# Tile 0 of a two-layer kernel: its last column group as seven quarter products, with another order of weight loads and of the second layer

## The chip, the cores and the metric

The kernel runs on one core of one Trainium2 chip. The metric is the device time of one execution in microseconds (us). Before the change the median of three runs is 261.32 us (261.23 to 261.98). A difference of about 0.3% (0.8 us) is what can be told from no change.

## What is computed

Linear attention without softmax over 8 batches of 8 heads (576 positions, 64 features), a normalisation of each output row, and two dense layers with a gate between them:

```python
kv  = einsum('bhsd,bhse->bhde', k, v)
out = einsum('bhsd,bhde->bhse', q, kv)
x   = out / sqrt(mean(out*out, -1) + 1e-6) * g_norm   # rows of 8 heads x 64 = 512 features
h   = x @ w_in            # 4608 x 512  times 512 x 2048
g   = h * sigmoid(1.702 * h)
y   = g @ w_out           # 4608 x 2048 times 2048 x 512
```

Inputs and output are float32 in HBM; the kernel works in float16 with float32 sums in PSUM.

## The kernel before

**Tiles.** The 4608 rows are worked in nine tiles of 512: tile t (0 to 7) takes positions 0 to 511 of batch t, and tile 8 the remaining 64 positions of all batches. While a tile goes through the two layers, the attention of the next batch is spread between its matmuls. Every engine's order is written out by hand: `layers` (L789) runs the first layer, then the second, and after step i of either it calls the units that the main loop (L978 to L1059) registered with `at1(i, ...)` and `at2(i, ...)`. Nothing is reordered later, so each engine works through its instructions in the order of the calls.

**Tiles 1 to 8** use a Strassen-like scheme in both layers. The two operands are cut in quarters, and seven products of quarters take the place of eight. In the first layer `SevenIn` (L546) does it for a group of four 128-wide columns of the hidden layer (i, i+1, i+8, i+9): products 1 to 7 of four matmuls with 256 columns each. Products 1, 6, 7 and 4 add up in one PSUM bank, x; product 2 goes into bank y, which starts as ScalarE's or VectorE's copy of x after product 1 (L604); 5 and 3 go into bank z, and a copy of z after product 5 is kept in SBUF as s5 (L606). After products 5 and 6 VectorE adds x and s5 into z (L608); after product 7 it adds x to s5 (L610). So product 7, which goes on adding to x, waits until L608 has read x. The gates (gelu, ScalarE, L574) read y after product 2, z after 3, x after 4, and s5 after L610. The operands are sums of quarters of the weights (`w_in_sums`, L504, into `ws`) and of the input (`Sums.form`, L522, into `xS`), formed on VectorE.

**Tile 0** uses no such scheme. Its first layer takes the 16 columns one by one, four matmuls of 512 columns each (`Hidden.mm`, L484), with a gelu on ScalarE behind each column (L496). The first six columns (0, 1, 2, 3, 8, 9) stand between the pieces of batch 0's attention (L892 to L914); `first_columns` (L806) does the other ten in the order 10, 11, 4, 5, 6, 12, 13, 7, 14, 15. The second layer, `project_all` (L816), is 64 steps of one matmul with 512 columns, step (mo, fo) adding column fo of the hidden layer times row block fo of w_out to output block mo. Two of its four accumulators come from the PSUM pool ps_h (three banks, tag hT), two from ps_o.

**Batch 1's attention** stands in tile 0's second layer, as units at steps: `pack_q` (VectorE puts q in order, L420), `q` (four transposes on PE into a ps_a bank, then ScalarE's copy, L425), `kv` (12 small matmuls per pair of heads, L248), `out` (one matmul, then ScalarE's square, L299), `ss` (one matmul that sums the squares into a ps_h bank, then ScalarE's reciprocal square root `rs`, L358), `apply` (VectorE multiplies into xT, L370). Gelu and the reciprocal square root lie in different ScalarE table sets; `preload_act_table_set` (step 4) loads one ahead of its use, and where an activation needs a set that isn't there, the compiler puts a load ahead of it. xT must be there when tile 1 begins.

**Loads.** All big loads go through GpSimd's queue (POOL), in the order of the calls: the rest of batch 0, w_in in seven pieces (L180 to L186, the last two being columns 4 to 7 and 12 to 15), then w_out and batch 1 in turn (L915 to L925). Eight of them are under way at a time: the ninth is issued when the first has landed. Since tile 1 on wants w_in multiplied by g_norm (`scale_w_in`, L203) and tile 0 unscaled, VectorE scales each part of w_in after tile 0 has used it and then forms the `ws` sums.

Of the kernel before, what the change touches and what calls it, by code (L numbers as in the profile page):

```python
# [16 lines left out]
def kernel(  # L17
# [10 lines left out]
    nc = tc.nc  # L28
# [14 lines left out]
    PE_ = 96  # L43
    NJ = S // PE_
    GROUP = 6
    COLS = (0, 1, 2, 3, 8, 9, 10, 11, 4, 5, 6, 12, 13, 7, 14, 15)
    assert PE_ * NJ == S and PE_ % 32 == 0

    const = ctx.enter_context(tc.tile_pool(name="const", bufs=1))
# [144 lines left out]
    def load_w_out(f0, f1):  # L194
        nc.gpsimd.dma_start(
            out=w_out_sb[:, f0:f1, :],
            in_=moe_w_out[f0 * P : f1 * P, :].rearrange("(fo ki) n -> ki fo n", ki=P),
        )
# [302 lines left out]
        lower = slice(KH + k.start, KH + k.stop)  # L501
        return w[:, k, f], w[:, lower, f], w[:, k, hi], w[:, lower, hi]

    def w_in_sums(g0, g1):  # L504

        f = slice(2 * g0 * P, 2 * g1 * P)
        a11, a12, a21, a22 = quarters(w_in_sb, f, slice(0, KH))
        s = [ws[:, n, :, f] for n in range(4)]
        nc.vector.tensor_add(s[0], a21, a22)
        nc.vector.tensor_sub(s[1], s[0], a11)  # L510
        nc.vector.tensor_sub(s[2], a11, a21)
        nc.vector.tensor_sub(s[3], a12, s[1])

    class Sums:

# [273 lines left out]
    def layers(t, units1, units2):  # L789
        hid = d0 if t == 0 else Hidden(t)  # L790
        seven = Seven(t, hid.gT) if t else None
        left = hid_seven(t, hid, seven, units1) if t else first_columns(hid, units1)
        osbs[t] = opool.tile([P, 4, DM], F32, name="osb", tag="osb")
        if t:
            todo = {n: [lambda x=x: seven.sums(*x) for x in xs] for n, xs in plan(t).later.items()}
            for n, us in units2.items():
                todo.setdefault(n, []).extend(us)
            for n, us in left.items():
                todo[n] = us + todo.get(n, [])
            seven.run(todo)  # L800
        else:
            project_all(hid.gT, units2)
        if t < B and t not in HALVED:
            store(t, 0, J)

    def first_columns(hid, units):  # L806

        for i, fo in enumerate(COLS):
            if i >= GROUP:
                for ko in range(KO):  # L810
                    hid.mm(ko, fo)
                hid.gate(fo)
            for u in units.get(i, ()):
                u()

    def project_all(gT, units):  # L816

        os = {}

        def project(mo, fo):  # L820
            if fo == 0:
                pool, tag = (ps_h, "hT") if mo < 2 else (ps_o, "o")
                os[mo] = pool.tile([P, DM], F32, name="o", tag=tag)
            nc.tensor.matmul(  # L824
                os[mo],
                gT[:, fo, mo * P : (mo + 1) * P],
                w_out_sb[:, fo, :],
                start=(fo == 0),
                stop=(fo == FO - 1),
            )  # L830
            if fo == FO - 1:
                copy = nc.scalar.copy if mo % 2 else nc.vector.tensor_copy
                copy(osbs[0][:, mo, :], os[mo])

        steps = [(mo, 4 * i + k) for i in range(3) for mo in range(4) for k in range(4)]
        steps += [(mo, f + k) for f in (12, 14) for mo in range(2) for k in range(2)]
        steps += [(mo, 12 + k) for mo in (2, 3) for k in range(4)]
        for n, (mo, fo) in enumerate(steps):
            project(mo, fo)
            for u in units.get(n, ()):  # L840
                u()
# [69 lines left out]
    for fo in COLS[4:GROUP]:  # L911
# [5 lines left out]
    load_w_out(4, 8)  # L917
    early_load("k", 1, 0, 2)
    load_w_out(8, 10)
    load_w_out(10, 12)  # L920
    early_load("v", 1, 0, 2)
    load_w_out(12, 14)
    early_load("k", 1, 2, NPAIR)
    early_load("v", 1, 2, NPAIR)
# [1 line left out]

    made = {}
    osbs = {}
    SECOND = Plan(
# [48 lines left out]
    for t in range(NT):  # L978
# [11 lines left out]

        if t == 0:
            for l in range(2):
                at1(6, nc.vector.memset, kvd[l], 0.0)
            at1(7, scale_w_in, 0, 4)
            at1(7, w_in_sums, 0, 2)
            at1(8, start, 1)
            at1(12, scale_w_in, 4, 6)
            at1(12, w_in_sums, 2, 3)
            at1(13, load_q, 2)
            at2(4, nc.scalar.preload_act_table_set, "abs_reciprocal_sqrt_and_small")  # L1000
            at2(18, weight_sum, 0, 0, HF)
            at2(18, scale_w_in, 6, 8)
            at2(18, w_in_sums, 3, 4)
            for c in range(NPAIR):
                at1(12, of(1, "pack_q", c))
                at2(9 + 3 * c, of(1, "q", c))
                at2((36, 37, 49, 50)[c], of(1, "kv", c))
                at2((41, 43, 54, 55)[c], of(1, "out", c))
                at2((45, 50, 58, 60)[c], of(1, "ss", c))
                at2((48, 52, 58, 62)[c], of(1, "apply", c))  # L1010
            for n in range(1, 4):
                at2(19, weight_sum, n, 0, 4)
                at2(38, weight_sum, n, 4, 6)
            at2(39, load_kv, 2, 0, H // 2, False)
            at2(51, clear_rest)
            at2(51, load_kv, 2, H // 2, H)

            def first_sum():
                made[1] = Sums(1, xT[1])
# [70 lines left out]
```

## Time and profile before

| | |
|---|---|
| median of three runs | 261.32 us |
| the profiled execution, its own time | 262.05 us |
| its span, first to last instruction | 260.3 us |
| around the span | 1.75 us |
| granted TensorE clock | 0.997 |
| tile 0's first layer (PE, from column 0's last quarter) | 16.99 to 28.21 us |
| tile 0's second layer with batch 1's attention | 28.21 to 47.52 us |
| tile 1's first product | 47.52 us |

Times in the views are microseconds from the span's start. A row of the timeline gives the start, the length of a run of like instructions, the engine, the line, output and inputs, their shape and count, and in brackets the engine's idle time ahead of it with what ended it. Matmuls overlap, so a run's length is longer than its distance to the next row: where PE is busy, the distance between starts is the price of a run. In the waits view a line gives who waited for whom, and the total, the count and the longest.

### The profile page before, as it was taken

What the parts mean: (1) busy time and instruction counts of PE and PEld (TensorE: products, weight loads), DVE (VectorE), ACT (ScalarE), POOL (GpSimd) and SP (SyncE); (2) the same over time, 40 slices, a digit from 0 to 9 for tenths busy, and PEclk for the clock granted to TensorE, in tenths of its full rate; (3) what the DMA queues carried; (4) which work ended last, traced back from release to release, by engine and by line L of the source; (5) the groups of instructions that cost most, each with busy time, mean ns of one, the idle gap of its engine ahead of it and who ended that gap; (6) DMA issues with size and microseconds to landing.
All of it is one profiled execution on the core that took longest, in us unless ns stands there. A gap on an engine that the chain in (4) does not pass through costs nothing.

```text
span 260.3 us, 6081 instructions
## 1 busy us (share of the span) xinstructions
PE 252.1 (97%) x2475; PEld 205.9 (79%) x2475; DVE 194.0 (75%) x350; ACT 174.1 (67%) x313; POOL 56.4 (22%) x85
## 2 busy tenths in 40 slices
PE   8899989999999999999999999999999999999992
PEld 2444544788988988898889888988899888888882
DVE  1656566899968986898689958995899578467831
ACT  2487714988649964996499649964897569737810
POOL 8963335107034002500160017200000000000000
PEclk9999999999999999999999999999999999999998
DMA  7999999999999969993799869998601620021005
GB/s 172 194 193 204 203 203 196 248 154 138 175 147 183 224 90 160 160 209 62 169 90 231 115 159 121 232 111 145 156 3 23 153 91 3 0 103 60 4 0 161
DMA packets 69886, 35.42 MB, mean 136 GB/s; under 512 B 39330, under 2 KB 67746, under 8 KB 69602
## 3 DMA queue, kind: packets, MB, share of 16 engines
q0 software_dynamic: 39056, 18.19, 55.8%
q1 hardware_dynamic: 30480, 16.45, 30.2%
q8 instruction: 19, 0.31, 0.5%
q10 hardware_dynamic: 322, 0.39, 0.5%
q14 instruction: 9, 0.07, 0.1%
HBM read 36.70 MB, written 9.44 MB: 177 GB/s over the span
## 4 chain that ended last, share of the span: by engine, by line
PE 84%; DMA 10%; POOL 4%; issue 0%; DVE 0%; POOLq 0%
PE h L594 38%; PE o L716 38%; DMA vbuf<-in_v_dram 6%; DMA w_in_sb<-in_moe_w_in_dram 4%; PE o L824 2%; PE outR L308 2%; PE kvp L236 2%; POOL w_in_sb L170 1%; POOL qraw L99 1%; POOL kraw L101 1%; POOL vbuf L101 1%; PE ss L356 1%; PE kvp L248 1%; PE outT L281 0%; PE outT L285 0%
## 5 line engine op out<-in xcount | busy, mean ns | idle before, releaser
L574 ACT ACTIVATE gT<-h 128x512 f16<-128x512 f32 x96 | 52.8, 604 | 5.4 <-PE h L594 5.4
L594 PEld LDWEIGHTS <-ws 128*128 128x128 f16 x512 | 50.1, 98 | 5.8
L716 PEld LDWEIGHTS <-gS 128*128 128x128 f16 x512 | 49.7, 98 | 5.8
L594 PE MATMUL h<-xS,ws 128*128 128x256 f16 x384 | 52.2, 273 | 0.0
L716 PE MATMUL o<-tw,gS 128*128 128x256 f16 x384 | 46.4, 273 | 0.0
L594 PEld LDWEIGHTS <-w_in_sb 128*128 128x128 f16 x384 | 37.1, 98 | 4.7
L716 PEld LDWEIGHTS <-gT 128*128 128x128 f16 x384 | 37.0, 98 | 4.0
L716 PE MATMUL o<-w_out_sb,gT 128*128 128x256 f16 x256 | 33.5, 273 | 0.0
L594 PE MATMUL h<-xT,w_in_sb 128*128 128x256 f16 x224 | 31.9, 273 | 0.0
L691 DVE TENSOR_TENSOR osb<-o,qf 128x512 f32<-128x512 f32 (+1 forms) x25 | 16.7, 669 | 14.7 <-PE o L716 11.9
L608 DVE TENSOR_TENSOR h<-h,s 128x512 f32<-128x512 f32 x32 | 22.2, 698 | 6.7 <-PE h L594 5.5
L113 POOL DMA_DIRECT2D kraw<-in_k_dram x7 | 6.0, 852 | 92.7 <-PE kvp L236 87.4
L610 DVE TENSOR_TENSOR s<-h,s 128x512 f32<-128x512 f32 x32 | 22.1, 691 | 4.1 <-PE h L594 3.3
L646 DVE TENSOR_TENSOR gS<-gT 128x512 f16<-128x512 f16 (+2 forms) x32 | 21.7, 685 | 0.6 <-ACT gT L574 0.6
L574 ACT ACTIVATE gT<-s 128x512 f16<-128x512 f32 x32 | 19.8, 628 | 2.6 <-DVE s L610 2.6
L986 ACT ACT_TABLE_LOAD x15 | 19.2, 1283 | 0.3
L358 ACT ACTIVATE rs<-ss,eps_t 128x512 f32<-128x512 f32 (+1 forms) x14 | 8.2, 597 | 16.6 <-PE ss L356 16.6
L745 POOL DMA_DIRECT2D out_dram<-osb x2 | 1.1, 554 | 84.1 <-DVE osb L691 84.1
L594 PE MATMUL h<-xS,w_in_sb 128*128 128x256 f16 x128 | 18.9, 273 | 0.0
L544 ACT COPY h<-h 128x512 f32<-128x512 f32 x27 | 15.7, 585 | 2.1 <-PE h L594 2.0
L594 PE MATMUL h<-xT,ws 128*128 128x256 f16 x112 | 16.8, 273 | 0.0
L544 ACT COPY s<-h 128x512 f32<-128x512 f32 x18 | 10.6, 588 | 8.8 <-PE h L594 8.2
(105 smaller groups left out, 374.2 us busy)
## 6 DMA issues: line engine op xcount, KB each, us to landing
out_dram<-osb SPq DMA_DIRECT2D x12, 512.0 KB, 3.1
kraw<-in_k_dram POOLq DMA_DIRECT2D x5, 512.0 KB, 8.2
vbuf<-in_v_dram POOLq DMA_DIRECT2D x5, 512.0 KB, 11.5
qraw<-in_q_dram POOLq DMA_DIRECT2D x4, 512.0 KB, 13.6
out_dram<-osb SPq DMA_DIRECT2D x2, 1024.0 KB, 5.2
qbuf<-in_q_dram POOLq DMA_DIRECT2D x3, 512.0 KB, 12.7
w_in_sb<-in_moe_w_in_dram POOLq DMA_DIRECT2D x2, 512.0 KB, 10.4
w_out_sb<-in_moe_w_out_dram POOLq DMA_DIRECT2D x2, 512.0 KB, 14.9
```

Source lines behind the costliest of these rows:

```text
L101: nc.gpsimd.dma_start(out=raw[n][0:PE_, c0:c1, :].rearrange("p c (l x) -> p (c l) x", l=2), in_=early_src(n, b, c0, c1),)
L113: nc.gpsimd.dma_start(out=kv_rows[n][:, h0 * RW : h1 * RW].rearrange("p (h x) -> p h x", x=RW), in_=srcs[n][b, h0:h1, 0:SM, :].rearrange(" ...
L358: nc.scalar.activation(rs[:, 0:n], t[:, 0:n], AFT.Abs_reciprocal_sqrt, bias=eps_t, scale=1.0 / D)
L544: (nc.vector.tensor_copy if engine == "D" else nc.scalar.copy)(to, src)
L574: nc.scalar.activation(self.gT[:, to, n * TH : (n + 1) * TH], src, AFT.Gelu_apprx_sigmoid)
L594: nc.tensor.matmul(bank[name][:, a], w, x, start=(p in (1, 5) and a == 0 and k == 0), stop=(k == KH - 1), skip_group_check=True,)
L608: nc.vector.tensor_add(bank["z"], bank["x"], self.s5)
L610: nc.vector.tensor_add(self.s5, bank["x"], self.s5)
L646: op(s[:, n, lo], a, b)
L691: nc.vector.tensor_add(o, ps, self.kept[with_][:, m])
L716: nc.tensor.matmul(o, a, w, start=(p in (1, 2, 5) and i == 0 and (mo == 0 or split)), stop=(i == HF - 1), skip_group_check=True,)
L986: u2.setdefault(i, []).append(lambda: f(*args))
```

## The change

Tile 0's columns 6, 7, 14 and 15 are no longer done one by one but as one group of `SevenIn`, with all its banks x and z from ps_a, y from ps_h, and both copies (x to y, z to s5) on ScalarE. `first_columns` now works through 10, 11, 4, product 1, 5, product 2, 12, 13, products 5, 6, 7; products 3 and 4 are units of the second layer at steps 3 and 7. The gate of product 2 stands behind that of column 12, the gates of products 4 and 7 behind product 4. The group's sums come first from unscaled weights (`w_in_sums(3, 4)` at step 7 of the first layer), and are formed again from scaled ones later. Two of the sums for groups 0 and 1, the clearing of kvd, the packing of q, the scaling of the later parts and batch 2's q load move to later units. The load of v for batch 1's first four heads moves ahead of that of w_out's rows 10 and 11. The second layer takes row blocks 0 to 3 and 4 to 7 for all four outputs, then 8 to 15 two at a time, and batch 1's units stand at other steps.

```diff
--- before.py
+++ after.py
@@ -43,7 +43,8 @@
     PE_ = 96
     NJ = S // PE_
     GROUP = 6
-    COLS = (0, 1, 2, 3, 8, 9, 10, 11, 4, 5, 6, 12, 13, 7, 14, 15)
+    COLS = (0, 1, 2, 3, 8, 9)
+    COLS_LATER = (10, 11, 4, "1", 5, "2", 12, 13, "5", "6", "7")
     assert PE_ * NJ == S and PE_ % 32 == 0
 
     const = ctx.enter_context(tc.tile_pool(name="const", bufs=1))
@@ -501,15 +502,19 @@
         lower = slice(KH + k.start, KH + k.stop)
         return w[:, k, f], w[:, lower, f], w[:, k, hi], w[:, lower, hi]
 
-    def w_in_sums(g0, g1):
+    def w_in_sums(g0, g1, which=range(4)):
 
         f = slice(2 * g0 * P, 2 * g1 * P)
         a11, a12, a21, a22 = quarters(w_in_sb, f, slice(0, KH))
         s = [ws[:, n, :, f] for n in range(4)]
-        nc.vector.tensor_add(s[0], a21, a22)
-        nc.vector.tensor_sub(s[1], s[0], a11)
-        nc.vector.tensor_sub(s[2], a11, a21)
-        nc.vector.tensor_sub(s[3], a12, s[1])
+        for n in which:
+            op, a, b = (
+                (nc.vector.tensor_add, a21, a22),
+                (nc.vector.tensor_sub, s[0], a11),
+                (nc.vector.tensor_sub, a11, a21),
+                (nc.vector.tensor_sub, a12, s[1]),
+            )[n]
+            op(s[n], a, b)
 
     class Sums:
 
@@ -799,19 +804,43 @@
                 todo[n] = us + todo.get(n, [])
             seven.run(todo)
         else:
+            for n, us in left.items():
+                units2[n] = us + units2.get(n, [])
             project_all(hid.gT, units2)
         if t < B and t not in HALVED:
             store(t, 0, J)
 
     def first_columns(hid, units):
 
-        for i, fo in enumerate(COLS):
-            if i >= GROUP:
+
+        xs = Sums(0, hid.x)
+        part = SevenIn(hid, xs, len(PARTS) - 1, FIRST)
+        gates = []
+        for i, fo in enumerate(COLS_LATER):
+            if isinstance(fo, str):
+                gate = part.product(int(fo))
+                if gate:
+                    gates.append(gate)
+            else:
                 for ko in range(KO):
                     hid.mm(ko, fo)
                 hid.gate(fo)
+            if fo == 5 or fo == 12:
+                while gates:
+                    gates.pop()()
+            if i == 0:
+                for n in range(4):
+                    xs.form(n)
             for u in units.get(i, ()):
                 u()
+
+        def late(p):
+            gates.append(part.product(p))
+            gates.pop()()
+            while p == 4 and gates:
+                gates.pop()()
+
+        return {3: [lambda: late(3)], 7: [lambda: late(4)]}
 
     def project_all(gT, units):
 
@@ -832,9 +861,8 @@
                 copy = nc.scalar.copy if mo % 2 else nc.vector.tensor_copy
                 copy(osbs[0][:, mo, :], os[mo])
 
-        steps = [(mo, 4 * i + k) for i in range(3) for mo in range(4) for k in range(4)]
-        steps += [(mo, f + k) for f in (12, 14) for mo in range(2) for k in range(2)]
-        steps += [(mo, 12 + k) for mo in (2, 3) for k in range(4)]
+        steps = [(mo, f + k) for f in (0, 4) for mo in range(4) for k in range(4)]
+        steps += [(mo, f + k) for f in range(8, FO, 2) for mo in range(4) for k in range(2)]
         for n, (mo, fo) in enumerate(steps):
             project(mo, fo)
             for u in units.get(n, ()):
@@ -917,8 +945,8 @@
     load_w_out(4, 8)
     early_load("k", 1, 0, 2)
     load_w_out(8, 10)
+    early_load("v", 1, 0, 2)
     load_w_out(10, 12)
-    early_load("v", 1, 0, 2)
     load_w_out(12, 14)
     early_load("k", 1, 2, NPAIR)
     early_load("v", 1, 2, NPAIR)
@@ -926,6 +954,7 @@
 
     made = {}
     osbs = {}
+    FIRST = Plan("", {}, {}, {1: "AAAA", 5: "AAAA"}, "D", "aaaa", "aaaa", {}, ())
     SECOND = Plan(
         "01 15 11 05 02 06 21 16 12 07 25 03 26 22 04"
         " 35 31 27 13 17 36 kv 32 24 23 14 37 33",
@@ -990,30 +1019,32 @@
 
         if t == 0:
             for l in range(2):
-                at1(6, nc.vector.memset, kvd[l], 0.0)
-            at1(7, scale_w_in, 0, 4)
-            at1(7, w_in_sums, 0, 2)
-            at1(8, start, 1)
-            at1(12, scale_w_in, 4, 6)
-            at1(12, w_in_sums, 2, 3)
-            at1(13, load_q, 2)
+                at1(10, nc.vector.memset, kvd[l], 0.0)
+            at1(1, scale_w_in, 0, 4)
+            at1(1, w_in_sums, 0, 2, (0, 1))
+            at1(2, start, 1)
+            at1(7, w_in_sums, 3, 4)
+            at1(10, w_in_sums, 0, 2, (2, 3))
+            at2(8, scale_w_in, 4, 6)
+            at2(8, w_in_sums, 2, 3)
+            at2(8, load_q, 2)
             at2(4, nc.scalar.preload_act_table_set, "abs_reciprocal_sqrt_and_small")
             at2(18, weight_sum, 0, 0, HF)
-            at2(18, scale_w_in, 6, 8)
-            at2(18, w_in_sums, 3, 4)
+            at2(19, scale_w_in, 6, 8)
+            at2(19, w_in_sums, 3, 4)
             for c in range(NPAIR):
-                at1(12, of(1, "pack_q", c))
+                at2(0, of(1, "pack_q", c))
                 at2(9 + 3 * c, of(1, "q", c))
-                at2((36, 37, 49, 50)[c], of(1, "kv", c))
-                at2((41, 43, 54, 55)[c], of(1, "out", c))
-                at2((45, 50, 58, 60)[c], of(1, "ss", c))
-                at2((48, 52, 58, 62)[c], of(1, "apply", c))
+                at2((39, 39, 54, 54)[c], of(1, "kv", c))
+                at2((44, 46, 57, 58)[c], of(1, "out", c))
+                at2((48, 51, 60, 62)[c], of(1, "ss", c))
+                at2((50, 54, 61, 63)[c], of(1, "apply", c))
             for n in range(1, 4):
-                at2(19, weight_sum, n, 0, 4)
-                at2(38, weight_sum, n, 4, 6)
+                at2(19, weight_sum, n, 0, 2)
+                at2(40, weight_sum, n, 2, 6)
             at2(39, load_kv, 2, 0, H // 2, False)
-            at2(51, clear_rest)
-            at2(51, load_kv, 2, H // 2, H)
+            at2(54, clear_rest)
+            at2(54, load_kv, 2, H // 2, H)
 
             def first_sum():
                 made[1] = Sums(1, xT[1])
```

## The prediction

> **What bounds the kernel now.** I read the page's busy shares and clock first, then the chain that ended last, PE's waits, the busy time by stage, and the timelines of tile 0. The page:
>
> ```profile
> PE 252.1 (97%) x2475; PEld 205.9 (79%) x2475; DVE 194.0 (75%) x350; ACT 174.1 (67%) x313; POOL 56.4 (22%) x85
> ```
>
> PE is busy 97% of the span, so what counts is PE's waiting time and its amount of work. The chain of waits, in order of time, says where the last wait is:
>
> ```profile
> 21.78 16.32 DMA vbuf<-in_v_dram
> 38.10 0.14 issue
> 38.24 0.38 PE kvp L248 x12
> ```
>
> The last link ahead of PE's unbroken stretch is the load of v for batch 1. PE's waits up to 62 us:
>
> ```profile
> PE idle L861 <- DVE one_t L191: 1.3, 1, 1.3
> PE kvp L248 <- DMA vbuf<-in_v_dram: 1.0, 1, 1.0
> PE kv L248 <- DMA vbuf<-in_v_dram: 0.9, 2, 0.6
> PE hT L487 <- DVE xT L366: 0.3, 1, 0.3
> ```
>
> Of 3.5 us of waiting only the 1.0 us for v lies inside tile 0's layers; the rest is batch 0's start, which the change leaves alone. By stage (28.2 to 38.2 and 38.2 to 47.5 are tile 0's second layer, the last row is tile 1; after the engines' busy times come the granted clock, the DMA share and GB/s):
>
> ```profile
> 28.20:38.20 10.00, 9.06 (x54) 4.42 (x52) 6.47 (x14) 4.23 (x6) 3.54 (x5) 1.00 1.27 204
> 38.20:47.50 9.30, 9.26 (x83) 4.37 (x84) 5.39 (x14) 5.04 (x9) 4.36 (x6) 1.00 1.44 196
> 47.50:74.20 26.70, 26.70 (x288) 23.73 (x287) 24.63 (x45) 20.54 (x37) 5.26 (x7) 1.00 1.22 173
> ```
>
> From 38.2 us PE has no slack: tile 1 is busy 26.70 of 26.70 us. Whatever shift PE has at the end of tile 0 goes to the end of the kernel undiminished. So I follow PE through tile 0, old against new, to the start of tile 1 (47.52). Its rows:
>
> ```profile
> 16.99 11.38 PE L487 MATMUL hT<-xT,w_in_sb 128*128 128x512 f16 x52 [0.27 <-DVE xT L366]
> 28.21 2.32 PE L824 MATMUL o<-w_out_sb,gT 128*128 128x512 f16 x10
> ...
> 32.98 0.39 PE L429 MATMUL q<-ident,qbuf 128*128 128x128 f16 x4
> 33.21 4.05 PE L824 MATMUL o<-w_out_sb,gT 128*128 128x512 f16 x18
> 38.24 0.38 PE L248 MATMUL kvp<-vbuf,kraw 96*64 96x64 f16 x12 [0.98 <-DMA vbuf<-in_v_dram]
> 38.55 0.39 PE L824 MATMUL o<-w_out_sb,gT 128*128 128x512 f16 x1
> 38.87 0.38 PE L248 MATMUL kvp<-vbuf,kraw 96*64 96x64 f16 x12
> 39.18 1.04 PE L824 MATMUL o<-w_out_sb,gT 128*128 128x512 f16 x4
> ...
> 42.52 0.38 PE L248 MATMUL kvp<-vbuf,kraw 96*64 96x64 f16 x12
> ...
> 47.52 0.60 PE L594 MATMUL h<-xT,w_in_sb 128*128 128x256 f16 x4
> 47.95 0.60 PE L594 MATMUL h<-xS,ws 128*128 128x256 f16 x4
> ...
> 56.82 0.82 PE L236 MATMUL kvp<-vbuf,kraw 128*64 128x64 f16 x40
> ```
>
> The first row gives a price per 512-column matmul: (28.21 - 16.99)/52 = 0.216 us. Rows 47.52 and 47.95 give 0.437/4 = 0.109 us for a quarter product's matmul. After v the old path stands at 39.18 + one matmul and the re-entry, 39.79, when steps 0 to 39 and kv 0 and 1 are done (a matmul behind a kv block costs 0.32, 38.55 to 38.87, so 0.10 of re-entry). A result can be read 0.16 us after its matmul's slot (0.38 against 0.22).
>
> **The change part by part.** ScalarE's and VectorE's prices:
>
> ```profile
> 17.47 3.77 ACT L496 ACTIVATE gT<-hT 128x512 f16<-128x512 f32 x7
> ...
> 40.47 1.24 ACT L299 ACTIVATE sq<-outT 128x512 f16<-128x512 f32 x2 [6.48 <-PE outT L281]
> 41.77 0.69 ACT L358 ACTIVATE rs<-ss,eps_t 128x512 f32<-128x512 f32 x1
> ...
> 48.72 0.59 ACT L544 COPY s<-h 128x512 f32<-128x512 f32 x1
> 49.19 0.60 ACT L544 COPY h<-h 128x512 f32<-128x512 f32 x1
> 49.81 1.28 ACT L983 ACT_TABLE_LOAD   x1
> 51.10 0.60 ACT L574 ACTIVATE gT<-h 128x512 f16<-128x512 f32 x1
> ```
>
> ```profile
> 17.00 1.02 DVE L983 MEMSET kvd<- 128x512 uint32 x2
> ...
> 24.24 0.68 DVE L512 TENSOR_TENSOR ws<-w_in_sb,ws 128x1024 f16<-128x1024 f16 x1
> ...
> 28.98 1.03 DVE L420 COPY qbuf<-qraw 128x512 f16<-128x512 f16 x4 [1.08 <-DMA qraw<-in_q_dram]
> ...
> 42.49 0.69 DVE L370 TENSOR_TENSOR xT<-outT,rs 128x512 f16<-128x512 f32 x1 [1.48 <-ACT rs L358]
> ...
> 50.75 1.29 DVE L608 TENSOR_TENSOR h<-h,s 128x512 f32<-128x512 f32 x2
> ```
>
> A queued gelu costs (3.77 - 0.60)/6 = 0.53 us of ScalarE, a copy from PSUM 0.59 (0.5 queued), a table load 1.28 with nothing around it (copy ends 49.79, load 49.81, gelu 51.10), the root 0.69. On VectorE an addition of a PSUM bank to s5 takes 0.69; a sum of 1024 elements 0.60 from start to start, going by the 0.68 of row 24.24 less the 0.09 by which two additions of 0.69 overlap in 1.29.
>
> *Work.* 16 matmuls of 0.216 (3.45 us) go, 28 of 0.109 (3.05) come: **-0.40**.
>
> *First layer.* The last ten columns began at 28.21 - 40 x 0.216 = 19.58. New: 10, 11, 4 end at 22.17, product 1 at 22.61, column 5 at 23.47; product 2 waits some 0.05 for ScalarE's copy of x, ends at 23.96; column 12 begins then (before: 23.90, so its load needn't come sooner), 13 ends at 25.69, product 5 at 26.12, product 6 at 26.56. Product 7 writes bank x, which VectorE must read first, and VectorE needs s5. ScalarE has the gelu of 12 at 25.01, product 2's gate at 25.54, the gelu of 13 at 26.07, and only then the copy into s5, 26.59 to 27.18; VectorE adds 27.2 to 27.9. Product 7 begins at 27.93 in place of 26.56: **+1.37**. Nothing is there to hide it: PE's queue behind it is the second layer. The ws and xS sums are ready (the last sum that product 7 needs by about 25.1).
>
> *ScalarE's tables.* The preload of the root's set stayed at step 4, and product 4's gate now comes after it, at step 7. ScalarE's built list, behind the copy into s5:
>
> ```
> gate of product 3 | load (preload) | load (gelu) | gate of product 4 | gate of product 7 |
> copies of q 0 to 3 | square 0, square 1 | load (root) | root 0, root 1 | ...
> ```
>
> The preload is now undone by a second load right behind it, and a third brings the root's set back ahead of root 0; before, one load at 29 us served all. PE leaves product 7 at 28.37, product 3 at 29.67, product 4 at 30.97, reaches q 0 at 31.40. There it waits **0.35** for VectorE: the clearing of kvd (1.02) and two sums (1.20) now stand behind product 7's addition (ends 29.27) and ahead of the packing of q. The gate of product 3 ends at 30.47, the loads at 33.06, the gate of product 4 at 33.67; it frees bank x for q 2, which would start at 33.49: **0.23** more. The gate of product 7 and the copy of q 0 end at 34.74, freeing the bank of q 3, due at 34.59: **0.20**. q 3 ends at 35.01 against 33.21: PE is 1.80 late.
>
> *Loads and kv.*
>
> ```profile
> vbuf<-in_v_dram POOLq DMA_DIRECT2D x1, 288.0 KB, 16.3
> ```
>
> v was issued at 21.78 and landed at 38.10; PE had reached it at 33.21 + 18 x 0.216 = 37.10, so the wait cost 1.14. New: 21 steps to step 39, 35.01 + 4.53 = 39.54. That is past 38.10 even if v had kept its place, so the wait goes, **-1.14**, whatever the order of loads does. v takes the turn one load earlier. Rows 10 and 11 of w_out take v's old turn, and land by about 38.1, the two being one turn apart in the same queue; they are first used at 40.2. kv 0 and 1 side by side (0.38 + 0.31) end at 40.23; with the next re-entry PE is 0.54 late. The two pairs side by side save **-0.20** of re-entries.
>
> *The roots.* Two of the three ps_h banks hold accumulators, so ss 1 needs the bank of ss 0, freed by root 0. Step 44 ends at 41.41, out 0 and 1 at 41.63 and 42.28, ss 0 at 42.93, step 51 at 43.57: ss 1 is due. ScalarE: square 1 ends at 43.07, the load at 44.36, root 0 at 45.06. ss 1 starts at 45.10: **+1.53**. Before, the set was loaded, and root 0 ended long ahead of ss 1. From 45.32: three steps, kv 2 and 3, three steps to 47.41; out 2 waits **0.09** for kvb, because apply 1 stands ahead of its copies on VectorE; then step 58, out 3, steps 59 and 60, ss 2, steps 61 and 62 to 49.23. ss 3 waits **0.36** for the copy of accumulator 1, which stands behind two squares (ends 49.55). ss 3 and step 63 end at **50.02**, against 47.52.
>
> *The rest* costs nothing as long as it stays off PE: VectorE's ten further sums lie in its idle time, and xT's last part is ready at 51.4 (ss 3's result at 49.97, root 0.69, apply 0.69), ahead of tile 1's fifth product, its first user, at 50.02 + 4 x 0.437 = 51.8. Batch 2's k and v loads wait for kv 2 and 3, at 45.97 in place of 42.52, so start up to 3.4 us later; tile 1 uses them from 56.82 + 2.5. The nearest is batch 2's transpose of q:
>
> ```profile
> 49.05 5.85 SPq L271 DMA_TRANSPOSE qTd<-qraw  x1
> ```
>
> ```profile
> qTd<-qraw SPq DMA_TRANSPOSE x1, 9.9
> ```
>
> ```profile
> 60.32 0.39 PE L308 MATMUL outR<-kvd,qTd 128*128 128x128 f16 x4
> ```
>
> It lands at 58.95, 1.37 ahead of its reader. Its issue follows tile 0's store and so slips 2.5 us with PE; the cover stays about 1.3.
>
> **Sum.** Walked: 50.02 - 47.52 = +2.50. By terms: -0.40 - 1.14 - 0.20 + 0.05 + 1.37 + 0.35 + 0.23 + 0.20 + 1.53 + 0.09 + 0.36 = +2.44; the 0.06 is rounding in the re-entries. The profiled execution would take 262.05 + 2.5 = 264.55. It lies 0.73 above the median of the runs, with 1.75 outside its span; on the median it is **263.8 us**, +0.96%. Bounds: the operations are all in the trace in the same shapes; what isn't is how these waits fall. Product 7's wait is 0.84 with ScalarE's copy one gelu earlier, 1.9 one later. ss 1's is 0.28 if the load ahead of root 0 is hidden, 1.6 at most. The small four are 0 to 1.4 together. I take the walked values, and let the likeliest case run from 262.8 to 264.6.
>
> The Trainium skill, page "ScalarE: Activation LUTs", section "What ACT_TABLE_LOAD costs", gives 1283 ns for the load and about 1380 ns of drain for each switch, 2.66 us together. The trace has the first figure (1.28) and not the second: 0.02 us lie between copy and load, none between load and gelu.
>
> **Rivals.**
>
> *Loads of tables are hidden* (ends not slower). Place: ScalarE between the gates of products 3 and 4, and ahead of root 0. For it: ScalarE is idle 30 to 40 us. Against it: PE waits for just what stands behind the loads. Priced at nothing, the waits for q 2 and q 3 go, ss 1 waits 0.28, out 2 nothing, and the walk ends at 48.25: +0.73, 262.05, within 0.3%. It decides from loads of under 0.1 us a piece.
>
> *The faster side:* product 7 doesn't wait either, if bank x were read before. Then only -0.40 - 1.14 - 0.20 and 0.7 to 1.0 of small waits are left: 260.4. Against it: the copy into s5 stands third in ScalarE's queue.
>
> *A second bound in tile 1.* Batch 2's k and v loads move up to 3.4 us later and run beside the transpose of q. If it lands 1.5 to 2.5 late, its cover of 1.37 is gone: 264.5 to 265.3 (taken at 265.0). For it: 9.9 us to landing, against 5.85 of the queue's own. Against it: the transpose slips by 2.5 too, so the overlap grows by under 1 us.
>
> *A switch costs more than its row.* If each of the three loads held ScalarE twice as long as its row, PE would lose 3 x 1.28 more: 267.6. Rows 49.81 and 51.10 speak against it, for the gelu follows the load at once. The drain that the Trainium skill's page "ScalarE: Activation LUTs" states would be such a mechanism.
>
> **How the numbers follow.** The walk: 0.74. Second bound: 0.09. Dearer switches: 0.03. Hidden loads: 0.09. Faster side: 0.05. The forecast is the walk's 263.8. 262.6 to 265.1 takes the walk's bounds and the second bound, and leaves out 0.17. About 0.3% (0.8 us, so 260.5 to 262.1) is what a measurement of this kernel can tell from no change: faster 0.03 (from the faster side's 0.05, whose 260.4 is close to the limit), same 0.09 (0.02 of the faster side, 0.07 of hidden loads, which lies close to the other limit), slower 0.88.
>
> **What would show it.** PE waits about 1.4 us ahead of product 7 (at 26.6) for VectorE's addition, and about 1.5 ahead of ss 1 (near 43.6) for ScalarE's root; no wait for v. ScalarE shows two loads in a row near 30.5 and one near 43.1. Tile 1's first product starts near 50.0, and from there PE has no wait. If ss 1 doesn't wait, the walk is wrong by 1.5; if product 7 doesn't, by 1.4; if w_out's rows 10 and 11 stop PE at step 40, the loads were misjudged.

## The result and the profile after

The changed kernel takes 264.7 us (median of 6 runs, 264.09 to 265.04), the kernel before beside it 261.63 us (6 runs, 261.23 to 262.58): a ratio of 1.0117, 95% interval 1.0095 to 1.014, so **3.07 us slower**. Forecast were 263.8 us and "slower". Its profiled execution took 265.0 us with a span of 263.2.

The page's busy line of the changed kernel:

```profile
PE 252.8 (96%) x2487; PEld 207.3 (79%) x2487; DVE 198.0 (75%) x360; ACT 176.9 (67%) x317; POOL 56.3 (21%) x85
```

PE has twelve instructions more (28 for 16) and is still the engine that is never free. PE's waits over the whole span:

```profile
PE ss L357 <- ACT rs L359: 1.4, 1, 1.4
PE idle L889 <- DVE one_t L192: 1.3, 1, 1.3
PE h L599 <- DVE h L613: 1.1, 1, 1.1
PE kv L249 <- DMA vbuf<-in_v_dram: 1.1, 2, 0.7
PE hT L488 <- DVE xT L367: 0.3, 1, 0.3
PE q L430 <- DVE qbuf L421: 0.2, 1, 0.2
```

Three lines are new: ss 1 waits 1.4 us for ScalarE's root, product 7 1.1 us for VectorE's addition, q 0 0.2 us for its packing. The wait for batch 1's v (`kvp`) is gone. The other three belong to batch 0's start. Nothing waits in tile 1 or later. The timeline of PE through tile 0:

```profile
17.88 5.34 PE L488 MATMUL hT<-xT,w_in_sb 128*128 128x512 f16 x24 [0.27 <-DVE xT L367]
...
26.56 1.04 PE L599 MATMUL h<-xS,ws 128*128 128x256 f16 x8
28.73 0.60 PE L599 MATMUL h<-xS,ws 128*128 128x256 f16 x4 [1.14 <-DVE h L613]
...
40.35 0.57 PE L249 MATMUL kvp<-vbuf,kraw 96*64 96x64 f16 x24
40.85 1.25 PE L853 MATMUL o<-w_out_sb,gT 128*128 128x512 f16 x5
...
43.45 0.81 PE L853 MATMUL o<-w_out_sb,gT 128*128 128x512 f16 x3
45.65 0.38 PE L357 MATMUL ss<-sq,ones 128*128 128x512 f16 x1 [1.39 <-ACT rs L359]
...
50.51 0.60 PE L599 MATMUL h<-xT,w_in_sb 128*128 128x256 f16 x4
```

Read slots, not only the brackets (a slot is what a matmul takes from start to start while PE is busy): eight product matmuls from 26.56 take 8 x 0.109 = 0.87, so product 7 was due at 27.43 and lost 1.30; three steps from 43.45 end at 44.10, so ss 1 lost 1.55. A measure for all that follows is **the path**: from the row that waits for xT (column 0's last quarter) to tile 1's first product. Here it is 50.51 - 17.88 = 32.63 us; in the profile of before that the prediction used it was 47.52 - 16.99 = 30.53. ScalarE on the same stretch:

```profile
27.34 0.60 ACT L549 COPY s<-h 128x512 f32<-128x512 f32 x1
30.66 0.60 ACT L579 ACTIVATE gT<-h 128x512 f16<-128x512 f32 x1 [2.72 <-PE h L599]
31.28 1.28 ACT L1015 ACT_TABLE_LOAD   x1
32.57 1.28 ACT L579 ACT_TABLE_LOAD   x1
33.86 0.60 ACT L579 ACTIVATE gT<-h 128x512 f16<-128x512 f32 x1
...
42.36 1.25 ACT L300 ACTIVATE sq<-outT 128x512 f16<-128x512 f32 x2 [5.44 <-PE outT L282]
43.62 1.28 ACT L359 ACT_TABLE_LOAD   x1
44.91 0.69 ACT L359 ACTIVATE rs<-ss,eps_t 128x512 f32<-128x512 f32 x1
```

The copy into s5 (27.34) ends at 27.94, and VectorE's addition starts at once; the root's set is fetched at 31.28, thrown out at 32.57 by the gate behind it, and fetched again at 43.62, so that root 0 ends at 45.60 where ss 1 was due at 44.10. Two loads in a row cost 33.86 - 31.28 = 2.58 us, 1.29 each, with nothing between or behind them. The Trainium skill, page "ScalarE: Activation LUTs", section "What ACT_TABLE_LOAD costs", gives about 1283 ns for the load, with which this agrees, and about 1380 ns of drain beside it, of which these rows show none.

### The profile page after: what moved, and what is told of

It is laid out like the page before. It is cut to its first block, busy times and chain, and to the rows that moved or that the text cites. A ratio compares the mean times of both kernels' runs of the same rounds, so it can differ in the third digit from the quotient of the medians.

```text
span 263.2 us, 6118 instructions
## 1 busy us (share of the span) xinstructions
PE 252.8 (96%) x2487; PEld 207.3 (79%) x2487; DVE 198.0 (75%) x360; ACT 176.9 (67%) x317; POOL 56.3 (21%) x85
## 4 chain that ended last, share of the span: by engine, by line
PE 88%; ACT 4%; DMA 2%; POOL 2%; DVE 1%; issue 1%
PE h L599 38%; PE o L721 37%; PE hT L488 3%; PE o L853 3%; DMA vbuf<-in_v_dram 2%; PE outR L309 2%; PE kvp L237 2%; PE ss L357 1%; ACT rs L359 1%; PE outT L282 1%; ACT sq L300 1%; POOL qraw L100 1%; POOL kraw L102 0%; ACT L359 0%; ACT L579 0%
## 5 line engine op out<-in xcount | busy, mean ns | idle before, releaser
L579 ACT ACTIVATE gT<-h 128x512 f16<-128x512 f32 x99 | 54.6, 604 | 8.2 <-PE h L599 8.1
L599 PEld LDWEIGHTS <-ws 128*128 128x128 f16 x528 | 51.7, 98 | 7.8 <-issue 1.3
L599 PE MATMUL h<-xS,ws 128*128 128x256 f16 x396 | 53.9, 273 | 1.1 <-DVE h L613 1.1
L599 PEld LDWEIGHTS <-w_in_sb 128*128 128x128 f16 x396 | 38.2, 98 | 5.5 <-issue 0.2
L599 PE MATMUL h<-xT,w_in_sb 128*128 128x256 f16 x232 | 33.1, 273 | 0.0
L613 DVE TENSOR_TENSOR h<-h,s 128x512 f32<-128x512 f32 x33 | 22.9, 697 | 8.9 <-PE h L599 5.8
L615 DVE TENSOR_TENSOR s<-h,s 128x512 f32<-128x512 f32 x33 | 22.8, 691 | 4.7 <-PE h L599 4.0
L579 ACT ACTIVATE gT<-s 128x512 f16<-128x512 f32 x33 | 20.5, 628 | 2.4 <-DVE s L615 2.4
L599 PE MATMUL h<-xS,w_in_sb 128*128 128x256 f16 x132 | 19.5, 273 | 0.0
L1015 ACT ACT_TABLE_LOAD x15 | 19.2, 1283 | 0.3
L549 ACT COPY h<-h 128x512 f32<-128x512 f32 x28 | 16.3, 587 | 1.9 <-PE h L599 1.8
## 6 DMA issues: line engine op xcount, KB each, us to landing
w_out_sb<-in_moe_w_out_dram POOLq DMA_DIRECT2D x2, 512.0 KB, 15.2
```

The costliest lines, as they stand in the source:

```text
L549: (nc.vector.tensor_copy if engine == "D" else nc.scalar.copy)(to, src)
L579: nc.scalar.activation(self.gT[:, to, n * TH : (n + 1) * TH], src, AFT.Gelu_apprx_sigmoid)
L599: nc.tensor.matmul(bank[name][:, a], w, x, start=(p in (1, 5) and a == 0 and k == 0), stop=(k == KH - 1), skip_group_check=True,)
L613: nc.vector.tensor_add(bank["z"], bank["x"], self.s5)
L615: nc.vector.tensor_add(self.s5, bank["x"], self.s5)
L1015: u2.setdefault(i, []).append(lambda: f(*args))
```

## The experiments

**e1_again**: the changed kernel once more, and **e5_before**, **e6_before**: the kernel before, two further profiles.

> The changed kernel itself, once more, for a second profile. From column 0's last quarter (PE's run of 512-column matmuls behind the wait for xT) to tile 1's first product PE took 30.53 us before (16.99 to 47.52) and 32.63 after (17.88 to 50.51): 2.10 of the 2.95 us between the two profiled executions. The other 0.89 lies in the opening, where the granted clock of the changed kernel was 0.50 to 0.88 from 10 to 16 us, in instructions that are the same in both kernels. If that dip is chance, the second profile shows 32.6 again (within 0.1) and an opening of 17.0 at a clock of 1.00 or another dip of another size. If the change itself brings the dip (another theory), it is there again at the same place, and the kernel stays 3 us slower, not 2.1.

> The kernel before, unchanged, for a second profile of it. Its first profiled execution took 262.05 us, the median of the 18 runs beside the last four kernels is 261.56, the lowest 260.78. Theory: that execution was one in which v landed late (38.10, a wait of 1.14 between slots); in a usual one v lands 0.3 to 0.9 us sooner and PE waits that much less, so that from column 0's last quarter to tile 1 it takes 29.7 to 30.2 us, not 30.53, and the 2.10 us between the two first profiles becomes 2.4 to 2.9. Rival: the wait for v is 1.1 again, and the spread of the runs lies in the opening, ahead of column 0's last quarter, or outside the span.

> The kernel before once more, as a third profile: the same expectations as for the second. Three profiles show whether the landing of v moves against PE from one execution to the next.

e1_again: 264.46 us (264.25 to 264.59), ratio 1.0109 [1.0088, 1.013]; waits 1.4, 1.1 and 0.2 as above; path 49.81 - 17.18 = 32.63, the same to the hundredth. The changed kernel's path repeats. That of before doesn't. e6_before's PE timeline where the prediction's profile had 0.98 us of idling for v:

```profile
17.00 11.40 PE L487 MATMUL hT<-xT,w_in_sb 128*128 128x512 f16 x52 [0.27 <-DVE xT L366]
...
33.23 4.05 PE L824 MATMUL o<-w_out_sb,gT 128*128 128x512 f16 x18
37.20 0.38 PE L248 MATMUL kvp<-vbuf,kraw 96*64 96x64 f16 x12
37.52 0.39 PE L824 MATMUL o<-w_out_sb,gT 128*128 128x512 f16 x1
...
45.03 0.59 PE L824 MATMUL o<-w_out_sb,gT 128*128 128x512 f16 x2
45.62 0.38 PE L356 MATMUL ss<-sq,ones 128*128 128x512 f16 x1
...
46.48 0.60 PE L594 MATMUL h<-xT,w_in_sb 128*128 128x256 f16 x4
```

PE goes from its 18 steps (they end at 37.12) into kv 0 at 37.20 without a wait. v was issued at 21.82 and took 15.2 us in place of 16.3: it landed at 37.02, 0.1 us ahead of PE. The path is 46.48 - 17.00 = 29.48. In e5_before it is 29.74, no wait for v either; its run of 52 matmuls takes 11.65 us there against 11.40, for w_in. Single times: 261.02 (e6_before) and 261.39 us (e5_before). So of three profiled executions of before one has the wait for v, and the loss by path is 32.63 - 29.48 = 3.15, where the medians differ by 3.07 (and by 2.90 for e1_again).

**e2_table**: the root's table is fetched behind the gates, so there is one load in place of three.

```diff
-            at2(4, nc.scalar.preload_act_table_set, "abs_reciprocal_sqrt_and_small")
+            at2(7, nc.scalar.preload_act_table_set, "abs_reciprocal_sqrt_and_small")
```

> The preload of the root's table set moves from step 4 to step 7 of the second layer, behind the gates of products 4 and 7; nothing else. Theory of the walk: one load in place of three on ScalarE; the waits ahead of q 2 and q 3 go (0.2 and 0.1), ss 1 waits 0.3 in place of 1.4, so tile 1's first product comes 1.7 us sooner: 30.9 from column 0's last quarter, and some 1.7 us (0.65%) less than the changed kernel. Rival: ss 1 waits for its bank because ss 0 and ss 1 stand only three steps apart, whatever the tables do; then the wait stays over 1 us and the gain is under 0.7 us.

262.87 us (262.62 to 263.45), ratio 1.0049 [1.0029, 1.0069]: 1.6 us less than e1_again. ScalarE:

```profile
31.95 0.60 ACT L579 ACTIVATE gT<-h 128x512 f16<-128x512 f32 x1 [0.70 <-PE h L599]
32.44 0.62 ACT L579 ACTIVATE gT<-s 128x512 f16<-128x512 f32 x1
33.08 1.28 ACT L1015 ACT_TABLE_LOAD   x1
...
43.29 0.69 ACT L359 ACTIVATE rs<-ss,eps_t 128x512 f32<-128x512 f32 x1
```

One load, behind both gates; the root follows the squares with none ahead of it. The waits of q 2 and q 3 are gone, and ss 1's falls from 1.55 to 0.29 between slots, about what the theory left of it. The path is 31.40, with 0.36 between slots of a wait for w_in that the changed kernel's two executions did not have: 31.04, or 1.59 less. The loads were not hidden: they cost what their rows say.

**e3_product7**: one column is done between product 6 and product 7, and VectorE, not ScalarE, copies z into s5. The group's sums are formed one place sooner, as product 5 comes sooner.

```diff
-    COLS_LATER = (10, 11, 4, "1", 5, "2", 12, 13, "5", "6", "7")
+    COLS_LATER = (10, 11, 4, "1", 5, "2", 12, "5", "6", 13, "7")
...
-    FIRST = Plan("", {}, {}, {1: "AAAA", 5: "AAAA"}, "D", "aaaa", "aaaa", {}, ())
+    FIRST = Plan("", {}, {}, {1: "AAAA", 5: "AAAD"}, "D", "aaaa", "aaaa", {}, ())
...
-            at1(7, w_in_sums, 3, 4)
+            at1(6, w_in_sums, 3, 4)
```

> Products 5 and 6 move ahead of column 13, so that this column stands between product 6 and product 7, and the copy of bank z into s5 goes to VectorE; nothing else. Theory of the walk: product 7 waits for the addition that reads bank x, which waits for the copy; the wait falls from 1.1 us of idle (1.3 between slots) to 0.2 to 0.4, so about 1 us (0.4%) less than the changed kernel. Rival: PE is delayed there by ScalarE's gates of column 12 and product 2 holding PSUM banks; then moving the products changes the wait by under 0.3 us.

263.61 us (263.16 to 265.45), ratio 1.0086 [1.0057, 1.0116]; path 48.73 - 16.93 = 31.80, 0.83 less. In PE's timeline:

```profile
24.74 1.04 PE L599 MATMUL h<-xS,ws 128*128 128x256 f16 x8
25.62 1.03 PE L488 MATMUL hT<-xT,w_in_sb 128*128 128x512 f16 x4
26.96 0.60 PE L599 MATMUL h<-xS,ws 128*128 128x256 f16 x4 [0.32 <-DVE h L613]
```

Of product 7's 1.14 us of idling 0.32 are left (0.48 between slots), and ss 1 still waits 1.39: the two causes are separate. What helped is the column in between, which is 0.86 us of work for PE. From the end of product 5 to product 7 it is 26.96 - 25.18 = 1.78 us here and was 28.73 - 27.00 = 1.73 before this edit, so the copy on VectorE shortened nothing. The copy on ScalarE had started 0.34 us behind product 5 (27.00 to 27.34), this one 0.20 (25.38): ScalarE's queue ahead of the copy was worth no more than 0.14 of product 7's 1.30. The rest is the copy and the addition themselves, 1.30 us, and the hand-offs around them (0.20 ahead of the copy, 0.09 behind), of which product 6 covers only 0.44.

**e4_both**: the edits of e2_table and e3_product7 together.

> Both edits together: the preload at step 7, and products 5 and 6 ahead of column 13 with the copy on VectorE. Theory of the walk: the two waits lie one behind the other on PE and add: about 2.7 us (1.0%) less than the changed kernel; 29.9 to 30.2 from column 0's last quarter to tile 1, which is 0.3 to 0.6 less than before. Rival: a new bound (the load of v, or the packing of q on VectorE) takes over when PE comes sooner; then the sum is short by what PE waits there, and no better than before.

261.96 us (12 runs, 261.69 to 262.45), ratio 1.0015 [0.9998, 1.0032]; path 47.26 - 17.06 = 30.20. The savings add up: 1.59 + 0.83 = 2.42, measured 2.43 by the path and 2.50 by the medians. What is left above 29.48 are small waits (between slots 0.48 at product 7, and 0.28 to 0.35 each at q 0, ss 1, out 2 and ss 3), less the 0.40 of work saved and what the pairs of kv save. The expected gain over before was reckoned from the one profile of it that has the wait for v; against e6_before the path is 0.72 longer.

**e7_noseven**: the new order of loads and of the second layer without the seven products: all ten later columns one by one.

```diff
-    COLS_LATER = (10, 11, 4, "1", 5, "2", 12, 13, "5", "6", "7")
+    COLS_LATER = (10, 11, 4, 5, 6, 12, 13, 7, 14, 15)
...
-        return {3: [lambda: late(3)], 7: [lambda: late(4)]}
+        return {}
```

> The changed kernel without the seven products: tile 0's ten columns one by one as before, so no xS, no unscaled sums, no late products and only one load of the root's set in the second layer; the order of loads, of the second layer's steps and of batch 1's units as changed. Theory of the walk: no wait for v, kv 0 and 1 (2 and 3) side by side, some 0.2 each of waiting at ss 1 and ss 3: 29.7 to 30.0 us from column 0's last quarter to tile 1, 0.5 to 0.8 under the first profile of before and 2.6 to 2.9 under the changed kernel; 261.0 to 261.6. The whole loss is then the seven products' own waits, and the 0.40 us of matmuls that they save is less than what they cost even with both edits. Rival: the new order of loads or units has a price of its own; then this is slower than before by over 0.5 us.

261.33 us (12 runs, 261.0 to 263.74), ratio 0.9995 [0.9973, 1.0017]; path 46.95 - 17.16 = 29.79. Level with before: the other two parts of the change cost and bring nothing that can be told. All of the loss comes with the seven products. The three small waits at ss 1, out 2 and ss 3 are there without them (0.28 to 0.32 between slots).

**e8_oldloads**: the changed kernel with w_out's rows 10 and 11 ahead of v again.

```diff
-    early_load("v", 1, 0, 2)
     load_w_out(10, 12)
+    early_load("v", 1, 0, 2)
```

> The changed kernel with the loads in the order of before (w_out's rows 10 and 11 ahead of v); nothing else. Theory of the walk: PE reaches kv 0 at about 39.7, after v's landing at 38.1 in either order, so nothing changes: within 0.2 us of the changed kernel, and no wait for v. Rival: the moved load is what takes the wait for v away; then PE waits for v 0.5 to 1.1 us again and the kernel is that much slower.

264.57 us (264.22 to 264.83), ratio 1.0111 [1.0087, 1.0134]; no wait for v; path 32.88, of which 0.25 is a longer first run (w_in again). The order of v and w_out has no effect here, since PE reaches kv at 40.1 us and v landed at 37.7 (issued at 22.45, 15.2 us).

**e9_later7** and **e11_later7_again** (one kernel): the seven products with room behind each. Products 7, 3 and 4 are all units of the second layer, s5 is copied by VectorE, the table is fetched behind the last gate, q is packed ahead of the sums, and batch 1's units stand further apart; kv 2 and 3, and with them batch 2's later loads of k and v, move from step 54 to step 52. **e10_units**: e7_noseven with that spacing. The lines below are the main ones of e9's edit.

```diff
-    COLS_LATER = (10, 11, 4, "1", 5, "2", 12, 13, "5", "6", "7")
+    COLS_LATER = (10, 11, 4, "1", 5, "2", 12, 13, "5", "6")
...
-        return {3: [lambda: late(3)], 7: [lambda: late(4)]}
+        return {5: [lambda: late(7)], 7: [lambda: late(3)], 10: [lambda: late(4)]}
...
-            at2(4, nc.scalar.preload_act_table_set, "abs_reciprocal_sqrt_and_small")
+            at2(10, nc.scalar.preload_act_table_set, "abs_reciprocal_sqrt_and_small")
...
-                at2((44, 46, 57, 58)[c], of(1, "out", c))
-                at2((48, 51, 60, 62)[c], of(1, "ss", c))
+                at2((43, 45, 56, 58)[c], of(1, "out", c))
+                at2((47, 52, 59, 62)[c], of(1, "ss", c))
```

> The seven products kept, with each of their additions given a longer lead: product 7 is moved from ahead of the second layer to its step 5, products 3 and 4 to steps 7 and 10, s5 is copied by VectorE, the root's table is fetched at step 10 behind the gates, and the units of tile 1's attention are spread two steps further. Theory (the loss is made of waits on ScalarE and VectorE only, and the change saves 0.40 us of products): PE shows no wait of over 0.2 us from tile 0's last column to tile 1's first product, that path is 29.2 to 29.8 us (before, its two later executions: 29.48 and 29.74), the time 0.1 to 0.4 us under before's. Rival (with the waits gone the loads become the bound: v's second half and w_out's last rows, issued behind the added work): a wait of 0.3 to 0.8 us for one of them between 41 and 47 us, path 29.8 to 30.4, time level with before or up to 0.5 us above it.

> The kernel of e7_noseven with the same wider spread of tile 1's attention units (out at steps 43 and 45, 56 and 58; ss at 47, 52, 59 and 62). Theory: the three waits of some 0.2 to 0.3 us that e7 still showed (ss 1, out 2, ss 3) go, so the path falls from 29.79 us to about 29.2 and the time is 0.3 to 0.6 us under before's. Rival: the slots were lost to loads or to ScalarE's copies that stay where they are, and the path and time stay at e7's (29.8, 261.3).

e10_units: 261.14 us (12 runs), ratio 0.9996 [0.9977, 1.0015]; path 46.65 - 17.07 = 29.58, with a wait for w_in in it:

```profile
17.07 4.48 PE L488 MATMUL hT<-xT,w_in_sb 128*128 128x512 f16 x20 [0.27 <-DVE xT L367]
21.77 7.10 PE L488 MATMUL hT<-xT,w_in_sb 128*128 128x512 f16 x32 [0.22 <-DMA w_in_sb<-in_moe_w_in_dram]
```

Twenty matmuls end at 17.07 + 4.31 = 21.38, so that wait cost 0.39 between slots. Without it the path is 29.19, 0.6 below e7's and as expected. The expected 0.3 to 0.6 us in the times didn't come: they can't be told from before.

e9_later7: 261.57 us (12 runs, 260.69 to 262.84), ratio 1.0007 [0.9991, 1.0023]. Tile 1's first product starts at 46.12, earlier than in any run so far; of the waits in tile 0's layers only 0.31 us at ss 3 and 0.13 at kv 2 are left, between slots. Yet the time is level: neither theory nor rival had said where. The two rows of PE that tell it, from batch 2's products of k and v:

```profile
55.38 0.32 PE L237 MATMUL kvp<-vbuf,kraw 128*64 128x64 f16 x8
56.72 0.69 PE L237 MATMUL kvp<-vbuf,kraw 128*64 128x64 f16 x32 [1.03 <-DMA vbuf<-in_v_dram]
```

And the chain that ended there, in order of time:

```profile
33.75 12.08 DMA qraw<-in_q_dram
45.83 0.28 issue
46.12 10.56 DMA vbuf<-in_v_dram
56.68 0.04 issue
56.72 0.69 PE kvp L237 x32
```

v's last 64 KB could not be issued until batch 2's q had landed, eight loads being under way (q issued at 33.75 and seven behind it). The loads had been a bound that PE's lateness covered, one tile further on than the rival put it.

> The kernel of e9_later7 unchanged, for a second profile. In e9's one profile, tile 1's first product stood at 46.12 us, but batch 2's first products of k and v waited 1.03 us at 56.7 for v's last 64 KB; that load had been issued at 46.12, when the load of batch 2's q (issued 33.75) landed, and took 10.56 us. Theory (this is where the saved time goes in every execution): the same wait appears again, 0.5 to 1.5 us, with the path to tile 1's first product near 29.3 and a time level with before. Rival (the wait is a matter of one execution, as the wait for v in the profile of before turned out to be): no wait at batch 2's products, and a span under 259.2 us with the same time over the rounds.

> The kernel of e9_later7 with batch 2's two 32 KB loads of q's remainder issued behind the loads of its k and v, in place of ahead of them. Theory (the 1.03 us are given back because v's last 64 KB cannot be issued before an earlier load lands, with eight loads under way): v's last load is issued by 45.0 us in place of 46.1, the wait of 1.0 us at batch 2's products falls to 0 to 0.3 us, and the time is 0.5 to 1.0 us under that of e11_later7_again, 260.4 to 260.9 where before is 261.3. Rival (the DMA engines are full, so an earlier issue only lengthens the transfer): v's last load still lands at 56 to 57 us and the time stays within 0.3 us of e11_later7_again. Second rival: the remainder of q, now last, holds up its transpose and PE waits there for as long.

e11_later7_again: 261.16 us (12 runs, 260.68 to 261.57), ratio 0.9984 [0.9969, 0.9999]; path 46.38 - 17.10 = 29.28, with a wait for w_in in it again:

```profile
17.10 4.48 PE L488 MATMUL hT<-xT,w_in_sb 128*128 128x512 f16 x20 [0.27 <-DVE xT L367]
21.84 1.04 PE L488 MATMUL hT<-xT,w_in_sb 128*128 128x512 f16 x4 [0.26 <-DMA w_in_sb<-in_moe_w_in_dram]
```

Between slots it cost 0.43 (21.84 - 21.41); without it the path is 28.85. Batch 2's 40 products take 56.73 - 55.65 = 1.08 us from start to start against 0.75 undisturbed: the wait is there again, at 0.33 us (v's last load issued 45.98, landed 56.07). It exists in both executions, but it is smaller than the 0.5 to 1.5 us expected; how large it is differs from one execution to the next.

**e12_rest_last**: the same kernel, with batch 2's two 32 KB loads of q's remainder behind its k and v. `load_q` has a new argument for it, which leaves the remainder out.

```diff
-            at2(8, load_q, 2)
+            at2(8, load_q, 2, False)
...
             at2(52, load_kv, 2, H // 2, H)
+            at2(52, load_q_rest, 2, qrem[0])
```

260.59 us (12 runs, 260.33 to 261.46), ratio **0.9965 [0.9949, 0.9981]**: faster than before by 0.9 us. Its POOL rows:

```profile
44.08 0.73 POOL L119 DMA_DIRECT2D kraw<-in_k_dram  x1
44.78 0.71 POOL L119 DMA_DIRECT2D vbuf<-in_v_dram  x1
45.46 1.27 POOL L139 DMA_DIRECT2D qrem<-in_q_dram  x2
```

and its PE rows:

```profile
17.15 5.34 PE L489 MATMUL hT<-xT,w_in_sb 128*128 128x512 f16 x24 [0.27 <-DVE xT L368]
...
46.00 0.60 PE L600 MATMUL h<-xT,w_in_sb 128*128 128x256 f16 x4
...
55.26 0.82 PE L238 MATMUL kvp<-vbuf,kraw 128*64 128x64 f16 x40
56.01 0.61 PE L600 MATMUL h<-xT,w_in_sb 128*128 128x256 f16 x4
```

v's last load goes out without a wait, 1.2 to 1.3 us sooner, and lands 6.5 us later in place of 10.1 to 10.6; the 40 products take 0.75. The rival that an earlier issue only lengthens the transfer is out, and the remainder of q holds nobody up. The path is 46.00 - 17.15 = 28.85, 0.63 below before's 29.48. The median lies 0.57 under e11's; the two intervals still overlap a little, so the step from e11 to e12 rests on the rows more than on the times. The new order of loads was not tried on the kernel before; its three profiles and e10's show no wait at batch 2's 40 products (0.75 to 0.76 us from start to start) that it could take away.

## Why the prediction was right, and where its numbers were off

Direction, place and kind of every wait were right: the two long ones, the table loads that make the one at ss 1, the lack of any effect of the load order, and no new wait in tile 1. By its own terms, against the path of e6_before:

| term | predicted | measured |
|---|---|---|
| work | -0.40 | -0.40 (4 quarter matmuls 0.43 to 0.44) |
| wait for v goes | -1.14 | 0 |
| pairs of kv side by side | -0.20 | -0.45 |
| product 2 | +0.05 | +0.03 |
| product 7 | +1.37 | +1.30 |
| q 0, q 2, q 3 | +0.35, +0.23, +0.20 | +0.34, +0.22, +0.13 |
| ss 1 | +1.53 | +1.55 |
| out 2 | +0.09 | +0.27 |
| ss 3 | +0.36 | +0.31, of which before has 0.16 |
| sum | +2.44 | +3.14 |

The measured column is 28.73 - 27.43 for product 7 and 45.65 - 44.10 for ss 1; the small ones are worked out in the same way, as a row's start less the end of the steps ahead of it. In the sum ss 3 counts with 0.31 - 0.16 = 0.15. The sum of 3.14 fits the paths' 3.15 and the medians' 3.07.

**The step that failed** is "the wait goes, -1.14". That the wait goes is true; that before has it is true only of the execution whose profile was at hand. The prediction saw the sign of it, "it lies 0.73 above the median of the runs", and then carried the whole difference over to the median. Without that term its sum is +3.58, 0.44 above the measured 3.14, and most of that is two terms. One is ss 3, which waits 0.16 in before too, and there the prediction had no wait. The other is the pairs, which were sized too small: two kv blocks side by side take 40.85 - 40.35 = 0.50 us for 24 matmuls, where the prediction had 0.38 + 0.31 and a re-entry; in e6_before two blocks cost 0.73 with theirs. That is -0.45 for both pairs. At the end 0.2 of it was eaten by out 2, which kvb holds up.

That the time still lay within 262.6 to 265.1 us was in part luck. The measured 264.7 is above the 264.6 at which the walk's likeliest case ends; the room above that was left for a second bound in tile 1, which didn't come. Of the 0.9 us between forecast and result 0.3 is the base: the median of before is 261.63 in six runs, where the first three gave 261.32. The bound of 0.84 us for product 7 with the copy one gelu earlier was not to be had either: by the prediction's own prices product 5's result can be read at 26.12 + 0.16 = 26.28, and a copy from there makes the wait 1.06.

**The rivals.** Hidden loads of tables: refuted by e2_table, 1.6 us. The faster side (product 7 doesn't wait): it idled 1.14, for want of work for PE between product 6 and product 7. The reason that the prediction gave, the copy's third place in ScalarE's queue, is the small part of it: 0.14 us by the rows of e3_product7, where 0.86 us of work in between took 0.82 off the wait. The second bound in tile 1 didn't appear in the changed kernel; e9 found one, but in v's last load and not in the transpose of q, and only for a kernel whose tile 1 starts 4 us sooner. Dearer switches: 1.29 us a piece in the rows, and e2_table's gain of 1.59 leaves no room for 1.28 more for each of the two loads that it saves.

**Where the expected gain went.** The seven products save 0.40 us of PE. Each of the group's gates, copies and additions is one more hand-off between engines that work in a fixed order. Three places paid for it: product 7, with a copy and an addition of 1.3 us to wait out and one product of 0.44 to cover them (1.30 between slots); q 2 and q 3, behind a gate behind two table loads (0.35); and ss 1, behind a root behind a third load (1.55, of which 0.29 stays without the load). With those hand-offs given room the work saved shows in the path: 28.85 in e11 (its 0.43 for w_in taken off) and in e12, against 29.19 for the same order without the seven products (e10_units, its 0.39 taken off). That is 0.34 of the 0.40, as a difference of single executions an estimate. In the times it is not shown by itself: e10's ratio to before is 0.9996 [0.9977, 1.0015] and e12's 0.9965 [0.9949, 0.9981], the intervals touch, and e12 has another order of loads besides.

## What to carry to other kernels

On an engine that is never free, a cut in its work is worth only what its new waits leave: walk every added hand-off through the fixed queue of the engine that gives it, count what work the busy engine has meanwhile, and look above all for an activation whose table a neighbour has just replaced. A wait in one profile is a property of that execution until a second profile shows it; if the profiled time lies well off the median, ask first whether the wait that you are about to save is the reason. When waits go away, follow the time on into the next stage: here a load that had been covered by lateness came due there.

## What the runs showed of the hardware beyond this

The first profile of the changed kernel reached column 0's last quarter 0.7 us later than e1_again, with the same instructions. Busy time by stretch (the columns as in the prediction, with the granted clock third from the end), first of the changed kernel's first execution:

```profile
10.00:12.00 2.00, 1.26 (x22) 0.53 (x16) 1.13 (x3) 1.00 (x3) 2.00 (x4) 0.88 1.34 197
12.00:14.00 2.00, 1.85 (x23) 1.18 (x23) 1.38 (x4) 0.88 (x2) 2.00 (x3) 0.50 1.23 199
14.00:16.00 2.00, 2.00 (x9) 0.75 (x7) 0.89 (x2) 1.28 (x2) 1.71 (x4) 0.76 1.37 196
```

then of e1_again:

```profile
12.00:14.00 2.00, 1.38 (x24) 0.86 (x24) 1.60 (x4) 1.07 (x3) 2.00 (x3) 1.00 1.23 198
```

If the clock was either full or half at each moment, it was half for some 3.4 us, an estimate (0.12 / 0.5 of the first 2 us, all of the second, 0.24 / 0.5 of the third: 0.48 + 2.00 + 0.96), in one execution and not in the other. The Trainium skill, page "TensorE: Matmul & The Clock Gate", Part 1, says that the clock is gated to half after an idle window of about 3.4 us that runs free of the kernel; the half agrees, and the dip is about one such window long, while PE was busy 1.52 of 2.00 us from 8 to 10 us and 1.26 from 10 to 12, so it was thinly used there and not idle. The dip falls ahead of the path and explains nothing of the 3 us.

The landing of one load differs by a microsecond and more between executions of one kernel: the same load of v took 16.3, 15.2 and 15.2 us from issue in three profiles of before.
